# The turned rest's last 64 features on TensorE's two row halves, and a block's five down sums in an order set per block

## The chip, the cores and the metric

The kernel runs on one core of one Trainium2 chip. The metric is device time in microseconds (us) of one execution. The text uses the profiler's names for the engines: PE is TensorE's matmul path, PEld its weight loads, DVE is VectorE, ACT is ScalarE, POOL is GpSimd and SP is SyncE, which here only issues DMAs.

## What is computed

Two branches read the same input `x` of 2048 tokens by 640 features and are mixed by a gate of one number per token:

```python
x = A_x
g = _sigmoid((x * gate_w).sum(-1, keepdims=True))
a = _A_ref(x, A_wqkv, A_w_phi, A_wo)      # linear attention, 32 heads of 20
b = _B_ref(x, B_w_gate, B_w_up, B_w_down) # (silu(x @ w_gate) * (x @ w_up)) @ w_down
return g * a + (1 - g) * b
```

In `_A_ref`, q and k go through a small matrix per head and then through softmax(p) and softmax(-p), side by side. `kv` and `z` are sums over all tokens of phi_k times v and of phi_k; the output is phi_q times `kv`, divided by phi_q times `z`, and projected by `wo`. All inputs are bfloat16. The middle width of `_B_ref` is 1728 = 13 x 128 + 64, so its last slice of features has 64 rows instead of 128.

## The kernel before

**Tiles.** Tokens are handled in 16 tiles of 128 (attention) and in 4 blocks of 512 (`bt`, the feed-forward branch). The feed-forward's middle features are 14 slices (`k`): 13 of 128 and slice 13 of 64. A *pair* is the gate and the up matmuls of one slice of one block, five of 512 columns each (`ffn`). ACT then takes a tanh and a scaled copy out of PSUM, DVE multiplies into `hT` (line 690), and POOL multiplies by the copy (line 699, `hmul`). Slice 13 is stored folded: rows 0 to 63 of `hT[:, hb, 13, 0:256]` hold its 64 features for the block's tokens 0 to 255, rows 64 to 127 hold the same features for tokens 256 to 511.

**Down.** Each block has five sums over the 14 slices. Four (`down`, u = 0 to 3) give the first 512 output features of 128 tokens each. The fifth (`rest`) gives the last 128 output features of all 512 tokens, *turned*: features on partitions, tokens on columns; ACT copies it out and a DMA turns it back. Slices 0 to 12 are thirteen full-height matmuls per sum. Slice 13 is done for the four `down` sums by `edge`: four matmuls of 512 columns that use 64 rows each, in the order 0, 2, 1, 3, so that the upper and the lower row half of the PE array work side by side. The turned rest instead ends with two full-height matmuls of 256 columns whose weights are half zeros: `wd[:, 13, 512:640]` (zeros below) for tokens 0 to 255 and `wr` (zeros above) for tokens 256 to 511. A sum that stands ahead of `edge` is *early*: it starts the PSUM bank and `edge` closes it. The others are started by `edge`.

**Attention.** A *k tile* is fifteen matmuls of 460, 481 and 500 columns into a pair of PSUM banks and one bank more. DVE follows with a maximum (line 1057), a minimum (1061) and two subtractions (1065, 1069); the second subtraction gives the pair of banks back. ACT takes the exponential, DVE a sum (1080) and a reciprocal (1084), POOL normalises (1090). A *q tile* does the same with 480 columns, then a DMA turns it, `num` multiplies by the kv matrix, DVE divides (1192), another DMA turns, and `wo` projects.

**Order.** A planner in the kernel (`_Plan`) fixes the order of all engines while the program is built. It walks through planned time with a list per engine, sorted by priority, and starts the first task whose inputs, buffers and PSUM banks are ready by its own costs. Tasks can be held to a planned time: k tile `t` at `K_AT + K_EACH*t`, q tile `t` at `Q_AT + Q_EACH*t`. The DMAs that turn tiles are given an allowance on top of their planned landing (`E_SLACK`, `O_SLACK`). `downs_of` lists a block's sums and `D_AFTER` says behind which slice of a later block they stand. On the chip each engine works its list in order and waits on semaphores. `_Order` leaves out waits of PE on its own semaphore.

Line 466 is the helper through which nearly all matmuls go, line 476 the same for most of ACT's work.

Of the kernel before, what the change touches and what calls it, by code (L numbers as in the profile page):

```python
# [6 lines left out]
P = 128  # L7
S_TOK = 2048
D = 640
H = 32  # L10
DH = 20
F_FFN = 1728
NT = S_TOK // P
NBT = S_TOK // 512
NK = 14
# [31 lines left out]
BF16 = DT.bfloat16  # L47
# [204 lines left out]
class _Plan:  # L252
# [100 lines left out]
def _mm(*cols):  # L353
    return sum(c / 2400.0 + 0.003 for c in cols)


def _build(
# [34 lines left out]
    wkv = sb("wkv", [P, 5, KVW], BF16)  # L392
    wo = sb("wo", [P, 5, D], BF16)
    wd = sb("wd", [P, NK, D], BF16)
    wr = sb("wr", [P, P], BF16)
# [50 lines left out]
    def one(b, c0, c1, r0=0, r1=P):  # L446
        return ps[r0:r1, b * 512 + c0:b * 512 + c1]
# [4 lines left out]
    def mms(groups):  # L452

        reads = [g[1] for g in groups] + [g[2] for g in groups]
        writes = []
        seen = set()
        for g in groups:
            k = (g[0].offset, str(g[0].ap))
            if k not in seen:
                seen.add(k)  # L460
                writes.append(g[0])

        def fn():
            last = None
            for o, l, r, st, sp_ in groups:
                last = pe.matmul(o, lhsT=l, rhs=r, start=st, stop=sp_, skip_group_check=True)  # L466
            return last
        run("pe", fn, reads=reads, writes=writes)

    def acc(o, pairs):  # L470
        n = len(pairs)
# [33 lines left out]
    v1pad = v1all.rearrange("p (g x) -> p g x", x=WIN)[:, :, WIN - 1]  # L505

    DM = 512
    L_SLACK, E_SLACK, O_SLACK = 1.0, 1.8, 1.6
    chain = {}

    def load(eng, dst, src, land, prio, transpose=False, name="load", cost=0.06):

        t = add(eng, cost, lambda: dma(eng, dst, src, transpose=transpose), prio=prio, lat=2.0, name=name)
        t.land = land
        t.slack = L_SLACK if land > 13 else 0.0
        t.after = chain.get(eng)
        chain[eng] = t
        return t
# [75 lines left out]
    wqT_l = load_wT(0, 51.0, -26, range(4))  # L594
    wd_l = [load("sp", wd[:, 0:13, :], rows(B_w_down[0:13 * P, :]), 58.5, -25),
            load("sp", wd[0:64, 13, :], B_w_down[13 * P:F_FFN, :], 59.0, -24),
            load("sp", wd[64:P, 13, 0:DM], B_w_down[13 * P:F_FFN, 0:DM], 59.3, -23.9),
            load("sp", wr[64:P, :], B_w_down[13 * P:F_FFN, DM:D], 59.5, -23.8)]
    wo_l = load("sp", wo[:, :, :], rows(A_wo), 61.0, -23)
    xl = [x_[4] for x_ in xs]  # L600

# [3 lines left out]
    table = add("act", 1.3, lambda: actop(us[:, 1, 0:1], us[:, 0, 0:1], ACTF.Tanh), deps=[zero], prio=-20, name="table")  # L605
    ones_t = add("dve", 0.4, lambda: memset(v1ones, 1.0, "dve"), prio=-19)
    pads_t = add("dve", 0.2, lambda: memset(v1pad, 0.0, "dve"), prio=-18.5)
    for z_ in (wd[64:P, 13, DM:D], wr[0:64, :]):
        wd_l[3].deps.append(add("dve", 0.2, lambda z_=z_: memset(z_, 0.0, "dve"), prio=-18))

    def build_wbd(c):
        nh = PHI_NH[c]
# [155 lines left out]
    store_t = {}  # L768
    gs_t = {}
# [64 lines left out]

    rest_c = {}

    def edge(bt, rank):
        hb = bt % 2
        c_ = down_c[bt] = [{} for _ in range(4)]
        acq = [("bank", c_[u], "ps") for u in range(4) if u not in EARLY[bt]] + ([("bank", c_[3], "p2")] if bt == NBT - 1 else [])  # L840

        def tile(u, key="ps", c0=0, c1=DM):
            r0 = 64 * (u // 2)
            return (one(c_[u][key], 0, c1 - c0), hT[r0:r0 + 64, hb, 13, P * (u % 2):P * (u % 2) + P], wd[r0:r0 + 64, 13, c0:c1], u)

        def fn():
            last = [tile(3)] if bt < NBT - 1 else [tile(3, "ps", 0, 384), tile(3, "p2", 384, DM)]
            mms([(o, l, r, u not in EARLY[bt], u in EARLY[bt]) for o, l, r, u in [tile(0), tile(2), tile(1)] + last])
        edge_t[bt] = add("pe", 0.63, fn, deps=[mult_t[bt, 13]] + wd_l, prio=rank, acq=acq, name="edge")

    def rest(bt, rank):
        ctx = {}
        rest_c[bt] = ctx
        hb = bt % 2
        first = 4 * bt < B_FIRST

        def fn():
            o = one(ctx["ps"], 0, 512)
            mms([(o, wd[:, k, DM:D], hT[:, hb, k, :], k == 0, False) for k in range(13)] +
                [(o[:, 256 * i:256 * i + 256], l, hT[:, hb, 13, 0:256], False, True) for i, l in enumerate((wd[:, 13, DM:D], wr[:, :]))])  # L860
        rest_t[bt] = r_ = add("pe", _mm(*([512] * 13 + [256] * 2)), fn, deps=[mult_t[bt, k] for k in range(NK)] + wd_l, prio=rank,
                              acq=[("bank", ctx, "ps")], name="rest")

        def rcp():
            actop(xb[:, ctx["xb"], 0:512], one(ctx["ps"], 0, 512), ACTF.Copy)
        e = add("act", 0.49, rcp, deps=[r_], prio=1, acq=[("xb", ctx, "xb")], rel=[("bank", ctx, "ps")], name="rcp")
        xs_ = xsb[:, 4 * bt:4 * bt + 4, DM:D]

        def turn():
            dma("sp", xs_ if first else rX[:, ctx["rX"], :, :], xb[:, ctx["xb"], 0:512], transpose=True)  # L870
        x_ = add("sp", 1.3, turn, deps=[e, wq_done[0]], prio=0.5, lat=2.1, acq=() if first else [("rX", ctx, "rX")], rel=[("xb", ctx, "xb")], name="rX")
        x_.slack = E_SLACK
        if first:
            def scaled():
                g_ = gs[:, 1, 4 * bt:4 * bt + 4]
                poolop(lambda: pool.tensor_tensor(xs_, xs_, g_.unsqueeze(2).to_broadcast([P, 4, P]), ALU.mult), [xs_, g_], [xs_])
            x_ = add("pool", 1.1, scaled, deps=[x_, gs_t[bt]], prio=0.6, name="rsc")
        rest_x[bt] = x_

    def down(bt, u, rank):  # L880
        t = 4 * bt + u
        ctx = down_c[bt][u]
        hb = bt % 2
        early = u in EARLY[bt]
        tk = slice(P * u, P * u + P)

        def part(key, c0, c1):
            return lambda: mms([(one(ctx[key], 0, c1 - c0), hT[:, hb, k, tk], wd[:, k, c0:c1], early and k == 0, not early and k == 12) for k in range(13)])
        n = DM if t < NT - 1 else 384
        d_ = add("pe", _mm(*[n] * 13), part("ps", 0, n), deps=[mult_t[bt, k] for k in range(13)] + wd_l, prio=rank,  # L890
                 acq=[("bank", ctx, "ps")] if early else (), name="down")
        down_t[bt, u] = d_
        if early:
            edge_t[bt].deps.append(d_)
            return t, ctx, [(edge_t[bt], "ps", 0, n)]
        d_.deps.append(edge_t[bt])
        if n == DM:
            return t, ctx, [(d_, "ps", 0, n)]
        second = add("pe", _mm(*[DM - n] * 13), part("p2", n, DM), prio=0.0, name="down")
# [342 lines left out]
        for half in range(2):  # L1242
            kvpart(bt, half, 1.0)
    def downs_of(bt):
        e = [("d", u, bt) for u in range(4)]
        return [("r", 0, bt)] + e[0:2] + [("x", 0, bt)] + e[2:]
    seq = [("f", k, bt) for k in range(K_PAIRS) for bt in range(2) if bt or k >= HD]
    seq += [("f", k, 0) for k in range(K_PAIRS, NK)]
    for bt in range(1, NBT):
        for k in range(K_PAIRS if bt == 1 else 0, NK):  # L1250
            seq.append(("f", k, bt))
            if k == K_PAIRS * (bt == 1) + D_AFTER:
                seq += downs_of(bt - 1)[:1]
            if k == K_PAIRS * (bt == 1) + D_AFTER + 1:
                seq += downs_of(bt - 1)[1:]
    seq += downs_of(NBT - 1)
    downs = []
    for i, (kind, j, bt) in enumerate(seq):
        if kind == "f":
            ffn(bt, j, 10.0 + 0.01 * i)  # L1260
        elif kind == "r":
            rest(bt, 10.0 + 0.01 * i)
        elif kind == "d":
            if bt not in edge_t:
                edge(bt, 10.0 + 0.01 * seq.index(("x", 0, bt)))
            downs.append(down(bt, j, 10.0 + 0.01 * i))
    for t in range(NT):
        qtile(t, 5.0 + 0.01 * t)
# [56 lines left out]
```

## Time and profile before

| | |
|---|---|
| median of 3 runs | 286.21 us (286.15 to 286.26) |
| the profiled execution | 285.67 us, of which the span of the trace is 284.0 us |
| PE busy | 279.0 us (98% of the span) |
| DVE, POOL, ACT busy | 226.5, 166.8, 153.3 us |
| granted TensorE clock | 1.000 |

In the timeline a row merges like instructions that follow each other: start, length, engine, line, operation, output<-inputs, rows*columns of the array, shape, count. The end of a matmul is modelled and includes its way through the array, so that a row's length is longer than its share of PE: the distance between the starts of two rows is what PE spends on the first. Some matmul records are missing from the trace, and a row may then count one too few.

### The profile page before, as it was taken

What the parts mean: (1) busy time and instruction counts of PE and PEld (TensorE: products, weight loads), DVE (VectorE), ACT (ScalarE), POOL (GpSimd) and SP (SyncE); (2) the same over time, 40 slices, a digit from 0 to 9 for tenths busy, and PEclk for the clock granted to TensorE, in tenths of its full rate; (3) what the DMA queues carried; (4) which work ended last, traced back from release to release, by engine and by line L of the source; (5) the groups of instructions that cost most, each with busy time, mean ns of one, the idle gap of its engine ahead of it and who ended that gap; (6) DMA issues with size and microseconds to landing.
All of it is one profiled execution on the core that took longest, in us unless ns stands there. A gap on an engine that the chain in (4) does not pass through costs nothing.

```text
span 284.0 us, 4497 instructions
## 1 busy us (share of the span) xinstructions
PE 279.0 (98%) x1671; PEld 137.1 (48%) x1700; DVE 226.5 (80%) x334; ACT 153.3 (54%) x272; POOL 166.8 (59%) x140
## 2 busy tenths in 40 slices
PE   8999999999999999999999999999999999999996
PEld 3444544544544454455444455454554544454443
DVE  0324469999999999799989989999998999756114
ACT  2555746887765446676545554575435556635410
POOL 4198614677656744448765495687495686954200
PEclk9999999999999999999999999999999999999999
DMA  7988997957000100000011023332855553455012
GB/s 172 259 131 156 271 212 148 228 154 158 14 16 14 32 16 14 14 16 14 20 21 23 1 53 60 62 63 57 118 107 149 117 144 70 85 106 150 4 37 92
DMA packets 74591, 25.41 MB, mean 89 GB/s; under 512 B 62665, under 2 KB 74569, under 8 KB 74569
## 3 DMA queue, kind: packets, MB, share of 16 engines
q1 hardware_dynamic: 73257, 25.10, 40.8%
q8 instruction: 13, 0.21, 0.3%
q10 hardware_dynamic: 1312, 0.03, 0.3%
q14 instruction: 9, 0.07, 0.1%
HBM read 8.46 MB, written 2.62 MB: 39 GB/s over the span
## 4 chain that ended last, share of the span: by engine, by line
PE 89%; DVE 8%; issue 1%; ACT 1%; POOL 0%; POOLq 0%
PE ps L466 87%; PE ps L649 2%; DVE sm L1080 1%; DVE mx L1057 1%; DVE hT L690 1%; DVE phi L1065 1%; DVE phi L1069 1%; DVE ob L1192 1%; DVE mn L1061 1%; DVE rc L1084 1%; ACT us L694 0%; POOL hT L699 0%; ACT hT L476 0%; DVE rd L1184 0%; DVE dn L1182 0%
## 5 line engine op out<-in xcount | busy, mean ns | idle before, releaser
L699 POOL TENSOR_TENSOR hT<-hT,us 128x512 bf16<-128x512 bf16 (+1 forms) x56 | 62.4, 1121 | 61.9 <-DVE hT L690 35.4
L1090 POOL TENSOR_TENSOR phi<-phi,rc 128x1680 bf16<-128x1680 bf16 (+1 forms) x32 | 77.5, 2423 | 31.5 <-DVE rc L1084 31.4
L466 PE MATMUL ps<-xT,wg 128*128 128x512 bf16 (+1 forms) x285 | 65.9, 364 | 1.0 <-issue 0.2
L466 PE MATMUL ps<-xT,wu 128*128 128x512 bf16 x257 | 63.6, 379 | 0.2
L690 DVE SCALAR_TENSOR_TENSOR hT<-hT,ps 128x512 bf16<-128x512 bf16 (+1 forms) x60 | 38.4, 645 | 27.9 <-ACT hT L476 24.1
L476 ACT ACTIVATE hT<-ps 128x512 bf16<-128x512 f32 (+1 forms) x60 | 33.8, 567 | 36.4 <-PE ps L466 36.2
L466 PE MATMUL ps<-wkv,xT 128*128 128x460 bf16 (+2 forms) x240 | 51.1, 366 | 0.2 <-DVE phi L1069 0.2
L1080 DVE TENSOR_REDUCE sm<-phi 128x84 f32<-128x1680 bf16 (+1 forms) x32 | 48.3, 1513 | 2.0 <-ACT phi L476 2.0
L466 PE MATMUL ps<-wd,hT 128*128 128x512 bf16 (+3 forms) x231 | 48.3, 366 | 0.3
L476 ACT ACTIVATE phi<-phi 128x1680 bf16<-128x1680 bf16 (+1 forms) x32 | 41.7, 1302 | 7.2 <-DVE phi L1069 7.0
L466 PEld LDWEIGHTS ps<-xT,wg 128*128 128x128 bf16 x300 | 28.1, 98 | 29.2 <-issue 1.4
L694 ACT ACTIVATE us<-ps 128x512 bf16<-128x512 f32 (+1 forms) x60 | 33.9, 568 | 13.9 <-PE ps L466 12.8
L466 PEld LDWEIGHTS ps<-xT,wu 128*128 128x128 bf16 x260 | 25.3, 98 | 30.9 <-DMA wu<-in_B_w_up_dram 0.5
L466 PEld LDWEIGHTS ps<-wkv,xT 128*128 128x128 bf16 x240 | 23.2, 98 | 24.9 <-DVE phi L1069 0.7
L466 PEld LDWEIGHTS ps<-wd,hT 128*128 128x128 bf16 (+1 forms) x238 | 21.3, 98 | 25.1 <-issue 1.0
L1057 DVE TENSOR_REDUCE mx<-ps 128x42 f32<-128x840 f32 (+1 forms) x32 | 26.7, 833 | 7.6 <-PE ps L466 7.4
L1069 DVE TENSOR_TENSOR phi<-mn,ps 128x840 bf16<-128x840 f32 (+1 forms) x32 | 26.3, 821 | 0.3
L1061 DVE TENSOR_REDUCE mn<-ps 128x42 f32<-128x840 f32 (+1 forms) x32 | 26.5, 828 | 0.0
L1065 DVE TENSOR_TENSOR phi<-ps,mx 128x840 bf16<-128x840 f32 (+1 forms) x32 | 26.3, 822 | 0.0
L476 ACT ACTIVATE xb<-ps 128x512 bf16<-128x512 f32 x16 | 9.5, 595 | 19.7 <-PE ps L466 19.7
L466 PE MATMUL ps<-wo,oT 128*128 128x512 bf16 x77 | 19.2, 379 | 0.1
L466 PE MATMUL ps<-wq,xT 128*128 128x480 bf16 x80 | 18.7, 366 | 0.1
(64 smaller groups left out, 209.3 us busy)
## 6 DMA issues: line engine op xcount, KB each, us to landing
out_dram<-xsb SPq DMA_DIRECT2D x15, 160.0 KB, 1.9
wd<-in_B_w_down_dram SPq DMA_DIRECT2D x1, 2080.0 KB, 9.5
wg<-in_B_w_gate_dram SPq DMA_DIRECT2D x2, 400.0 KB, 6.3
wu<-in_B_w_up_dram SPq DMA_DIRECT2D x2, 400.0 KB, 7.3
wo<-in_A_wo_dram SPq DMA_DIRECT2D x1, 800.0 KB, 5.3
wg<-in_B_w_gate_dram SPq DMA_DIRECT2D x2, 320.0 KB, 4.3
wu<-in_B_w_up_dram SPq DMA_DIRECT2D x2, 320.0 KB, 4.9
wkv<-in_A_wqkv_dram SPq DMA_DIRECT2D x1, 600.0 KB, 8.0
```

The costliest lines, as they stand in the source:

```text
L466: last = pe.matmul(o, lhsT=l, rhs=r, start=st, stop=sp_, skip_group_check=True)
L476: run("act", lambda: act.activation(o, i, func, scale=scale), reads=reads, writes=[o])
L649: last = pe.matmul(one(b, 0, 512), lhsT=ones_row[:, 0:P], rhs=ones_row[:, 0:512], start=True, stop=True, skip_group_check=True)
L690: dveop(lambda: dve.scalar_tensor_tensor(out=h, in0=h, scalar=1.0, in1=g_, op0=ALU.add, op1=ALU.mult), [h, g_], [h])
L694: run("act", lambda: act.activation(o_, u_, ACTF.Copy, scale=0.5), reads=[u_], writes=[o_] if k < 13 else [o_, u_])
L699: poolop(lambda: pool.tensor_tensor(h, h, u_, ALU.mult), [h, u_], [h])
L1057: dveop(lambda: dve.tensor_reduce(a, b, AX.X, ALU.max), [b], [a])
L1061: dveop(lambda: dve.tensor_reduce(a, b, AX.X, ALU.min), [b], [a])
L1065: dveop(lambda: dve.tensor_tensor(o_, a, b, ALU.subtract), [a, mx[:, ctx["st"], 0:nh]], [o_])
L1069: dveop(lambda: dve.tensor_tensor(o_, a, b, ALU.subtract), [b, mn[:, ctx["st"], 0:nh]], [o_])
L1080: dveop(lambda: dve.tensor_reduce(a, b, AX.X, ALU.add), [b], [a])
L1090: poolop(lambda: pool.tensor_tensor(a, a, b, ALU.mult), [a, r], [a])
```

## The change

- `wr`, its load and the two DVE memsets of zeros are gone. `wd[64:128, 13, :]` now holds the last 64 rows of `w_down` in all 640 columns, by one load where there were two.
- The rest's two full-height matmuls of 256 columns are replaced by two of 256 columns on 64 rows, `turned(0)` and `turned(64)`, which join `edge`. Its order is now: turned(0) on the upper half; 2 (lower), 0 (upper), 3 (lower), 1 (upper); turned(64) on the lower half. In the last block tile 3 is split into 384 and 128 columns, as before.
- PE waits on its own semaphore for the end of `turned(0)` ahead of `turned(64)`, which writes the other half of the same PSUM bank.
- `rest` and `down` share a helper, `sums`. `SUMS` sets the order of the five sums (-1 is the rest) and of `edge` ("x") for each block. Before, the rest, 0 and 1 stood ahead of `edge`, and 2 and 3 behind; now 0 and the rest stand ahead.
- Constants of the planner move: `E_SLACK` 1.8 to 2.2, `O_SLACK` 1.6 to 1.9, the holds of k and q tiles, the times of the weight products (`PRE_...`), `D_AFTER` 1 to 3 with the whole of `downs_of` in one place. The order on every engine changes with them.

```diff
-    L_SLACK, E_SLACK, O_SLACK = 1.0, 1.8, 1.6
+    L_SLACK, E_SLACK, O_SLACK = 1.0, 2.2, 1.9
...
-            load("sp", wd[64:P, 13, 0:DM], B_w_down[13 * P:F_FFN, 0:DM], 59.3, -23.9),
-            load("sp", wr[64:P, :], B_w_down[13 * P:F_FFN, DM:D], 59.5, -23.8)]
+            load("sp", wd[64:P, 13, :], B_w_down[13 * P:F_FFN, :], 59.3, -23.9)]
...
-    for z_ in (wd[64:P, 13, DM:D], wr[0:64, :]):
-        wd_l[3].deps.append(add("dve", 0.2, lambda z_=z_: memset(z_, 0.0, "dve"), prio=-18))
...
-    K_AT, K_EACH, Q_AT, Q_EACH = 29.00, 6.821, 136.36, 6.844
-    PRE_Q = 10.07
-    PRE_EACH = 2.0
+    K_AT, K_EACH, Q_AT, Q_EACH = 30.00, 6.722, 137.19, 6.955
+    PRE_Q = 10.14
+    PRE_EACH = 2.3
     PRE_AT = 23.6
-    PRE_X = 27.5
-    D_AFTER = 1
+    PRE_X = 27.0
+    D_AFTER = 3
     FIN_DVE = 12
-    EARLY = ((0, 1),) * NBT
+    SUMS = ((0, -1, "x", 1, 2, 3), (0, -1, "x", 1, 2, 3), (-1, 0, "x", 1, 2, 3), (0, -1, "x", 2, 1, 3))
...
+        def turned(r0):
+            return (one(c_[-1]["ps"], 4 * r0, 4 * r0 + 256), wd[r0:r0 + 64, 13, DM:D], hT[r0:r0 + 64, hb, 13, 0:256], -1)
...
         def fn():
             last = [tile(3)] if bt < NBT - 1 else [tile(3, "ps", 0, 384), tile(3, "p2", 384, DM)]
-            mms([(o, l, r, u not in EARLY[bt], u in EARLY[bt]) for o, l, r, u in [tile(0), tile(2), tile(1)] + last])
-        edge_t[bt] = add("pe", 0.63, fn, deps=[mult_t[bt, 13]] + wd_l, prio=rank, acq=acq, name="edge")
+            done = halves([turned(0)])
+            halves([tile(2), tile(0), last[0], tile(1)] + last[1:])
+            pe.wait_ge(tr.sem["pe"], done[1])
+            halves([turned(64)])
+        edge_t[bt] = add("pe", 0.74, fn, deps=[mult_t[bt, 13]] + wd_l, prio=rank, acq=acq, name="edge")
...
-            mms([(o, wd[:, k, DM:D], hT[:, hb, k, :], k == 0, False) for k in range(13)] +
-                [(o[:, 256 * i:256 * i + 256], l, hT[:, hb, 13, 0:256], False, True) for i, l in enumerate((wd[:, 13, DM:D], wr[:, :]))])
+        rest_t[bt], r_ = sums(bt, -1, 512, lambda: [(one(ctx["ps"], 0, 512), wd[:, k, DM:D], hT[:, hb, k, :]) for k in range(13)], rank)
...
     def downs_of(bt):
-        e = [("d", u, bt) for u in range(4)]
-        return [("r", 0, bt)] + e[0:2] + [("x", 0, bt)] + e[2:]
+        return [("d", j, bt) for j in SUMS[bt]]
```

More of the change, by code (lines that the diff above doesn't have):

```diff
@@ L394, in _build @@
     wd = sb("wd", [P, NK, D], BF16)
-    wr = sb("wr", [P, P], BF16)
     wg = sb("wg", [P, 5, F_FFN + 128], BF16)
@@ L467, in fn @@
             return last
-        run("pe", fn, reads=reads, writes=writes)
+        return run("pe", fn, reads=reads, writes=writes)
     def acc(o, pairs):
@@ L835, in _build, with early @@
     rest_c = {}
+    def early(bt, j):
+        return SUMS[bt].index(j) < SUMS[bt].index("x")
     def edge(bt, rank):
         hb = bt % 2
-        c_ = down_c[bt] = [{} for _ in range(4)]
-        acq = [("bank", c_[u], "ps") for u in range(4) if u not in EARLY[bt]] + ([("bank", c_[3], "p2")] if bt == NBT - 1 else [])
+        c_ = down_c[bt] = {j: {} for j in range(-1, 4)}
+        acq = [("bank", c_[j], "ps") for j in range(-1, 4) if not early(bt, j)] + ([("bank", c_[3], "p2")] if bt == NBT - 1 else [])
+        def turned(r0):
+            return (one(c_[-1]["ps"], 4 * r0, 4 * r0 + 256), wd[r0:r0 + 64, 13, DM:D], hT[r0:r0 + 64, hb, 13, 0:256], -1)
         def tile(u, key="ps", c0=0, c1=DM):
@@ L844, in tile, with halves, sums, fn @@
             return (one(c_[u][key], 0, c1 - c0), hT[r0:r0 + 64, hb, 13, P * (u % 2):P * (u % 2) + P], wd[r0:r0 + 64, 13, c0:c1], u)
+        def halves(l):
+            return mms([(o, l_, r, not early(bt, j), early(bt, j)) for o, l_, r, j in l])
         def fn():
             last = [tile(3)] if bt < NBT - 1 else [tile(3, "ps", 0, 384), tile(3, "p2", 384, DM)]
-            mms([(o, l, r, u not in EARLY[bt], u in EARLY[bt]) for o, l, r, u in [tile(0), tile(2), tile(1)] + last])
-        edge_t[bt] = add("pe", 0.63, fn, deps=[mult_t[bt, 13]] + wd_l, prio=rank, acq=acq, name="edge")
+            done = halves([turned(0)])
[3 more added lines that the diff above has]
+        edge_t[bt] = add("pe", 0.74, fn, deps=[mult_t[bt, 13]] + wd_l, prio=rank, acq=acq, name="edge")
+    def sums(bt, j, n, groups, rank):
+        ctx = down_c[bt][j]
+        def fn():
+            mms([(o, l, r, early(bt, j) and k == 0, not early(bt, j) and k == 12) for k, (o, l, r) in enumerate(groups())])
+        t_ = add("pe", _mm(*[n] * 13), fn, deps=[mult_t[bt, k] for k in range(13)] + wd_l, prio=rank,
+                 acq=[("bank", ctx, "ps")] if early(bt, j) else (), name="down" if j >= 0 else "rest")
+        if early(bt, j):
+            edge_t[bt].deps.append(t_)
+            return t_, edge_t[bt]
+        t_.deps.append(edge_t[bt])
+        return t_, t_
     def rest(bt, rank):
-        ctx = {}
+        ctx = down_c[bt][-1]
         rest_c[bt] = ctx
@@ L855, in rest @@
         first = 4 * bt < B_FIRST
-        def fn():
-            o = one(ctx["ps"], 0, 512)
-            mms([(o, wd[:, k, DM:D], hT[:, hb, k, :], k == 0, False) for k in range(13)] +
-                [(o[:, 256 * i:256 * i + 256], l, hT[:, hb, 13, 0:256], False, True) for i, l in enumerate((wd[:, 13, DM:D], wr[:, :]))])
-        rest_t[bt] = r_ = add("pe", _mm(*([512] * 13 + [256] * 2)), fn, deps=[mult_t[bt, k] for k in range(NK)] + wd_l, prio=rank,
-                              acq=[("bank", ctx, "ps")], name="rest")
+        rest_t[bt], r_ = sums(bt, -1, 512, lambda: [(one(ctx["ps"], 0, 512), wd[:, k, DM:D], hT[:, hb, k, :]) for k in range(13)], rank)
         def rcp():
@@ L883, in down @@
         hb = bt % 2
-        early = u in EARLY[bt]
         tk = slice(P * u, P * u + P)
         def part(key, c0, c1):
-            return lambda: mms([(one(ctx[key], 0, c1 - c0), hT[:, hb, k, tk], wd[:, k, c0:c1], early and k == 0, not early and k == 12) for k in range(13)])
+            return [(one(ctx[key], 0, c1 - c0), hT[:, hb, k, tk], wd[:, k, c0:c1]) for k in range(13)]
         n = DM if t < NT - 1 else 384
[L890 to L896, printed above, removed]
+        down_t[bt, u], d_ = sums(bt, u, n, lambda: part("ps", 0, n), rank)
         if n == DM:
             return t, ctx, [(d_, "ps", 0, n)]
-        second = add("pe", _mm(*[DM - n] * 13), part("p2", n, DM), prio=0.0, name="down")
+        second = add("pe", _mm(*[DM - n] * 13), lambda: mms([(o, l, r, False, k == 12) for k, (o, l, r) in enumerate(part("p2", n, DM))]),
+                     prio=0.0, name="down")
         second.after = d_
@@ L1252, in _build @@
             if k == K_PAIRS * (bt == 1) + D_AFTER:
-                seq += downs_of(bt - 1)[:1]
-            if k == K_PAIRS * (bt == 1) + D_AFTER + 1:
-                seq += downs_of(bt - 1)[1:]
+                seq += downs_of(bt - 1)
     seq += downs_of(NBT - 1)
@@ L1260, in _build @@
             ffn(bt, j, 10.0 + 0.01 * i)
-        elif kind == "r":
-            rest(bt, 10.0 + 0.01 * i)
-        elif kind == "d":
+        else:
             if bt not in edge_t:
-                edge(bt, 10.0 + 0.01 * seq.index(("x", 0, bt)))
+                edge(bt, 10.0 + 0.01 * seq.index(("d", "x", bt)))
+            if j == "x":
+                continue
+            if j < 0:
+                rest(bt, 10.0 + 0.01 * i)
+                continue
             downs.append(down(bt, j, 10.0 + 0.01 * i))
```

## The prediction

> **What bounds the kernel now.** I read the page first, for the share of each engine:
>
> ```profile
> span 284.0 us, 4497 instructions
> PE 279.0 (98%) x1671; PEld 137.1 (48%) x1700; DVE 226.5 (80%) x334; ACT 153.3 (54%) x272; POOL 166.8 (59%) x140
> PEclk9999999999999999999999999999999999999999
> PE 89%; DVE 8%; issue 1%; ACT 1%; POOL 0%; POOLq 0%
> ```
>
> PE is busy for 279.0 of 284.0 us at full clock and has 89% of the chain that ended last. A saving must therefore be PE work removed or a PE stall removed; any other engine counts only where it makes PE wait. Next, the view of waits, for the stalls that are left:
>
> ```profile
> PE ps L466 <- DVE phi L1069: 0.2, 1, 0.2
> PEld ps L466 <- DMA wu<-in_B_w_up_dram: 0.5, 1, 0.5
> PEld ps L466 <- POOL hT L699: 0.4, 1, 0.4
> ```
>
> Three waits, and no more. A row's modelled end hides a part of a stall, so I take their size from the starts in the timeline. The first two rows below are the place of the DVE wait, the other four the place of the POOL wait at the end of the last block:
>
> ```profile
> 80.28 1.24 PE L466 MATMUL ps<-xT,wu 128*128 128x512 bf16 x5
> 81.69 3.22 PE L466 MATMUL ps<-wkv,xT 128*128 128x460 bf16 x15 [0.16 <-DVE phi L1069]
> ...
> 260.97 1.24 PE L466 MATMUL ps<-xT,wu 128*128 128x512 bf16 x5
> 262.05 1.24 PE L466 MATMUL ps<-wo,oT 128*128 128x512 bf16 x5
> 263.13 1.25 PE L466 MATMUL ps<-xT,wg 128*128 128x256 bf16 x10
> 264.50 2.98 PE L466 MATMUL ps<-wd,hT 128*128 128x512 bf16 x13
> ```
>
> Five matmuls of 512 columns take 1.08 us (262.05 - 260.97), 0.216 each. At 80.28 they take 1.41, so the eighth k tile waits 0.33 us for DVE's second subtraction of the sixth. The ten matmuls of 256 columns of slice 13 begin at 263.13; at 0.109 each (next part) the first down sum could start at 264.22 and starts at 264.50, a wait of 0.28 us for POOL's product of slice 12. Everywhere else the pitches hold, so PE's list is nearly a fixed sum of matmuls.
>
> **The two half-empty matmuls.** What goes, four times, is a pair of 256 columns:
>
> ```profile
> L466 PE MATMUL ps<-hT,wr 128*128 128x256 bf16 x4 | 1.1, 273 | 0.0
> L466 PE MATMUL ps<-hT,wd 128*128 128x256 bf16 x4 | 1.1, 272 | 0.0
> ...
> 133.96 0.27 PE L466 MATMUL ps<-hT,wr 128*128 128x256 bf16 x1
> 134.07 0.86 PE L466 MATMUL ps<-v,phi 128*128 128x64 bf16 x24
> ```
>
> One lasts 273 ns but holds PE for 0.11 (134.07 - 133.96), so two are worth 0.22 us a block. What comes instead is seen from the edge of block 1, which stands between a q tile and a gate; the two rows ahead of it give a q tile's pitch:
>
> ```profile
> 155.83 1.18 PE L466 MATMUL ps<-wq,xT 128*128 128x480 bf16 x5
> 156.84 0.38 PE L466 MATMUL ps<-wd,hT 128*128 128x512 bf16 x1
> ...
> 149.21 1.18 PE L466 MATMUL ps<-wq,xT 128*128 128x480 bf16 x5
> 150.32 0.61 PE L466 MATMUL ps<-wd,hT 64*128 64x512 bf16 x4
> 150.85 1.25 PE L466 MATMUL ps<-xT,wg 128*128 128x512 bf16 x5
> ...
> L466 PE MATMUL ps<-wd,hT 64*128 64x512 bf16 x15 | 2.4, 382 | 0.0
> ```
>
> A q tile takes 1.01 us, so edge could start at 150.22 and starts at 150.32: 0.10 to enter the halves. The row of four lasts 0.61 and one alone 0.38, so the second pair starts 0.23 after the first: two pairs stream for about 0.45. The next full matmul starts at 150.85, 0.08 after that. Edge costs 0.63 in all. With the change each half streams 1280 columns (256 + 512 + 512 above, 512 + 512 + 256 below) instead of 1024: 0.11 more, one entry and one exit as before, 0.74. Per block -0.22 + 0.11 = -0.11 us, over four blocks **-0.44 us**. More than that isn't there, since both halves are full from end to end.
>
> Less is possible in two ways. First, the pieces no longer start in equal pairs. That halves needn't be in step shows in the last block, where 384 and 128 columns below lie beside 512 above:
>
> ```profile
> 275.40 0.33 PEld L466 LDWEIGHTS ps<-wd,hT 64*128 64x128 bf16 x5 [0.42 <-issue]
> 275.94 0.55 PEld L466 LDWEIGHTS ps<-wd,hT 128*128 128x128 bf16 x4 [0.21 <-issue]
> ...
> 108.19 0.12 PEld L466 LDWEIGHTS ps<-wd,hT 64*128 64x128 bf16 x4
> ```
>
> From the first row-half load to the next full load it takes 0.54 us, as against 0.53 (150.32 to 150.85) for four equal pieces: the split cost nothing. The last row shows that all four weights of an edge are loaded within 0.12 us, while the first pair, 0.22 long, still streams. The Trainium skill says otherwise (TensorE: Matmul & The Clock Gate, The mechanism): a weight load overlaps with matmuls in flight only where its row group differs from theirs, by which each further piece on a half would show its load. The trace disagrees, since the second pair starts 0.23 and not 0.33 us after the first.
>
> Second, the new wait. PE waits on `turned(0)`, and behind it stand `turned(64)` and everything else of PE's list. How soon the end of a matmul of 256 columns is seen:
>
> ```profile
> 271.31 0.27 PE L466 MATMUL ps<-hT,wr 128*128 128x256 bf16 x1
> 271.62 0.60 ACT L476 ACTIVATE xb<-ps 128x512 bf16<-128x512 f32 x1 [2.43 <-PE ps L466]
> ```
>
> ACT starts 0.31 us after that matmul's start. `turned(64)` comes up when `tile(1)` has begun, 0.11 + 0.22 = 0.33 after `turned(0)`, and the lower half is free for it at 0.44. So the wait should be over when PE reaches it, with 0.02 to 0.13 us to spare, and I take it at nothing. At worst it shows a bare weight load, the 0.10 of the entry, which would eat the whole 0.11 of its block.
>
> **The two waits that go.** They are not the change's subject, but it moves the order. The order as built puts, between the last up group of block 3 and its first down sum, a `num` (eleven short matmuls), two `wo` groups and slice 13: more than 2 x 1.08 + 1.09 = 3.25 us of PE, where there was one `wo` group and slice 13, 2.17. What POOL's product needs:
>
> ```profile
> 262.25 0.60 ACT L694 ACTIVATE us<-ps 128x512 bf16<-128x512 f32 x1 [0.48 <-PE ps L466]
> 263.30 1.15 POOL L699 TENSOR_TENSOR hT<-hT,us 128x512 bf16<-128x512 bf16 x1 [2.71 <-ACT us L694]
> ```
>
> From the end of the up group (262.05) over ACT's copy and POOL's product (to 264.45) to PE's start at 264.50 it takes 2.45 us. With 0.8 us to spare the wait is gone: **-0.28 us**. Were ACT or POOL later by more than that, the old price would be back; behind it the next late thing is the edge's need of slice 13, which has the sum of 0, that of the rest and a `wo` group ahead of it.
>
> The DVE wait, on the k tiles numbered from 0:
>
> ```profile
> 68.58 3.21 PE L466 MATMUL ps<-wkv,xT 128*128 128x460 bf16 x15
> 119.56 3.21 PE L466 MATMUL ps<-wkv,xT 128*128 128x460 bf16 x15
> 122.60 2.33 PE L466 MATMUL ps<-xT,wg 128*128 128x256 bf16 x15
> 71.83 1.03 DVE L1057 TENSOR_REDUCE mx<-ps 128x42 f32<-128x840 f32 x1
> 72.78 1.02 DVE L1061 TENSOR_REDUCE mn<-ps 128x42 f32<-128x840 f32 x1
> 80.61 1.02 DVE L1069 TENSOR_TENSOR phi<-mn,ps 128x840 bf16<-128x840 f32 x1
> 81.55 0.68 DVE L690 SCALAR_TENSOR_TENSOR hT<-hT,ps 128x512 bf16<-128x512 bf16 x1
> 82.15 1.02 DVE L1061 TENSOR_REDUCE mn<-ps 128x42 f32<-128x840 f32 x1
> 86.55 0.97 DVE L1069 TENSOR_TENSOR phi<-mn,ps 128x840 bf16<-128x840 f32 x1
> ```
>
> A k tile holds PE for 3.04 us (122.60 - 119.56). Before, k tile 5 starts at 68.58, its maximum at 71.83, and its second subtraction ends at 81.63: 9.8 us of DVE work, with the maximum of k tile 6 (0.95, from 71.83 to 72.78) within. In the new order that maximum stands behind, which leaves 8.85. Adding the pitches of the new PE order, with the DMA wait at the head kept, k tile 5 starts near 70.1; its maximum can start 3.25 us later as before, at 73.4, so the subtraction ends at 82.2. Between the two k tiles the order has one more k tile, two pairs, slice 13, both kv halves and a weight product, 13.0 us, so PE comes to k tile 7 at 83.1. It is 0.9 us early where it was 0.33 late: **-0.33 us**.
>
> What is late next is k tile 8, which waits for k tile 6's second subtraction. Before, 5.9 us lie between the ends of these two subtractions (81.63 to 87.52). The new order has two maxima and two products of line 690 more between them (0.95 and 0.60 each, the latter from 81.55 to 82.15): 9.0 us, which ends at 91.2, or up to 0.7 earlier as far as the gaps between rows in the older stretch close. PE gets there after another k tile, two pairs and two weight products, 7.8 us behind k tile 7: 90.9. That is 0.4 early to 0.3 late. So a new wait of 0 to 0.3 us is likely here, and I take **+0.15 us**, the middle, as nothing speaks for one end. Elsewhere on this path the new order leaves more: k tiles 9 to 11 and 13 to 15 stand 13 us and more behind the k tile whose banks they need, and k tile 12, at 8.9 us, comes when DVE has worked off its backlog, as 12 us without a new k tile lie ahead of k tile 10.
>
> **What costs nothing.** One load and two memsets go; the loads of `w_down` still stand ahead of the same work, first used 7 us later in the new order, and DVE's memsets stand at the very head, before its first product. The weight products for q move behind later pairs but number the same. The rest is now closed by edge, so its copy and its turn on SP's queue start later; in the last block a `wo` group and 52 matmuls of three sums still follow it on PE. q tiles start 2 to 3 us later (the first at 152.0 for 149.2), and so do `num` groups, but by the pitches the last q tile keeps its distance to its `num`, and the last `num` gets 0.7 us more to its `wo`. The end behind PE's last matmul (one DVE product, one store) is untouched.
>
> **Sum.** -0.44 - 0.28 - 0.33 + 0.15 = -0.90 us. The profiled execution of 285.67 us would become 284.77; it lies 0.54 below the median of 286.21, which I carry over: **285.3 us**. About 0.2%, 0.57 us, is what a measurement of this kernel can tell from no change, so 285.64 is the border to faster.
>
> **The rivals.** *The forecast* holds where edge saves its 0.44 and new waits stay below 0.47: 285.1 (none) to 285.64. Chance 0.67.
>
> *The waits only move.* DVE is busy for 80% of the span and paces the k tiles, q tiles start later with the same work behind, and any stretch may hold a new wait like the two that go. For it: the margin at k tile 8 is about nil. Against: the list of waits shows only these in 284 us, and turned tiles have larger allowances. With 0.61 us of new waits it is 286.21 - 0.44 = 285.77, the same by measurement; 286.1 with half as much again. Chance 0.16.
>
> *Weights of a half load in the open.* If the new order of unequal pieces loses the early loading, each half shows two loads of 0.10: edge is 0.94, the block loses 0.09, and with the waits as forecast it is 285.3 + 4 x 0.20 = 286.1. This is what the Trainium skill's rule above would do here. Against it stand the 0.12 us of the four loads and the unsplit cost of the last block. Chance 0.05.
>
> *The halves take turns.* If pieces overlap only where they start together, no two of the six do, since `turned(0)` shifts the upper half by 0.11. Then edge is 2560 columns in a row, 5 x 0.216 + 0.18 = 1.26, and a block loses 0.63 + 0.63 - 0.85 = 0.41 in place of gaining 0.11. Four times 0.52 on the forecast: 287.4, slower. It decides from 0.37 us per edge on. Against it: the last block's unequal edge of 0.54. Chance 0.07; another 0.05 for slower by several small things.
>
> **How the numbers follow.** Faster 0.67, same 0.16 + 0.05 = 0.21, slower 0.12. The range: below, 285.16 with no new wait, less a little for the spread of runs, 285.0; above, it takes in the moved waits and the open loads, 286.2, which leaves out the slower cases and little else.
>
> **What would show it.** Right: edge rows of six with 0.73 to 0.75 us from the pitch end before them to the next full matmul, and `wr` gone; no POOL wait near 264; the k tile near 83 unstalled; PE's list of waits of 0.5 us or less beside the one for the first `wu`. Wrong: a next full matmul 0.8 us or more behind the edge's first; a wait on PE's own semaphore with idle weight loads ahead of the last piece; rows of k tiles, `num` or `wo` with DVE, POOL or DMA as their releaser, which would say that the waits moved.

## The result, and the profile after

| | before | changed |
|---|---|---|
| median | 286.18 us (285.77 to 286.78, 10 runs) | 285.46 us (285.03 to 285.64, 10 runs) |
| ratio, 95% interval | | 0.9973 [0.9963, 0.9983] |
| the profiled execution | 285.67 us, span 284.0 | 285.48 us, span 283.7 |

The changed kernel is faster by 0.72 us (0.49 to 1.06 by the interval). A second measurement of it, further down, gives 0.9978 [0.9969, 0.9988]. The profiled execution itself is shorter by only 0.2 us, and that has to be explained as well.

In the changed kernel the line numbers are a little different: the helper for matmuls is line 465 (466 before), ACT's is 475, `hmul` is 695, DVE's second subtraction is 1078, its last products are 795 and 814 (799 and 818 before). SPq is SP issuing DMAs. First lines of the page of the changed kernel, and of its lists of waits for PE and for the weight loads:

```profile
span 283.7 us, 4489 instructions
PE 278.8 (98%) x1671; PEld 137.2 (48%) x1700; DVE 225.9 (80%) x332; ACT 152.5 (54%) x272; POOL 166.4 (59%) x140
PEclk9999999999999999999999999999999999999999
PE 98%; issue 1%; DVE 0%
...
PE ps L645 <- PEq L1318: 0.8, 1, 0.8
...
PEld ps L465 <- ACT us L690: 0.7, 2, 0.4
```

The chain that ended last passes through DVE only with the last product (0%) and no longer through POOL. PE's own list has one entry left, ahead of the first real matmul; the kernel before has the same one. A weight load that waits need not hold PE, so the waits that remain are read from the starts. First the edge of block 1, which now follows k tile 15, with the weight load of its last piece:

```profile
145.25 3.20 PE L465 MATMUL ps<-wkv,xT 128*128 128x460 bf16 x15
148.39 0.28 PE L465 MATMUL ps<-hT,wd 64*128 64x256 bf16 x1
148.39 0.71 PE L465 MATMUL ps<-wd,hT 64*128 64x512 bf16 x4
148.84 0.27 PE L465 MATMUL ps<-hT,wd 64*128 64x256 bf16 x1
149.04 2.76 PE L465 MATMUL ps<-wd,hT 128*128 128x512 bf16 x11
...
148.73 0.09 PEld L465 LDWEIGHTS ps<-hT,wd 64*128 64x128 bf16 x1
```

The k tile holds PE for 3.04 us, to 148.29. `turned(0)` starts 0.10 later, and the next full matmul at 149.04: the edge costs 0.75 by these rows, 0.74 by the unrounded starts, and 0.74 to 0.75 in each of the four blocks. `turned(64)`, the second row of 256 columns, starts at 148.84, 0.45 after `turned(0)`, which is when its half comes free. Its weights were loaded at 148.73, while the piece ahead of it on the same half still streamed.

Then the two places where PE stalled before, k tile 7 (and k tile 8, where a new wait was feared), with the DVE subtractions that give their banks back (and the maximum of k tile 5 ahead of them), and the end of block 3:

```profile
82.38 1.24 PE L465 MATMUL ps<-xT,wu 128*128 128x512 bf16 x5
83.46 3.20 PE L465 MATMUL ps<-wkv,xT 128*128 128x460 bf16 x15
...
90.19 1.24 PE L465 MATMUL ps<-xT,wu 128*128 128x512 bf16 x5
91.27 3.21 PE L465 MATMUL ps<-wkv,xT 128*128 128x460 bf16 x15
...
73.72 1.03 DVE L1066 TENSOR_REDUCE mx<-ps 128x42 f32<-128x840 f32 x1 [1.19 <-PE ps L465]
80.77 1.02 DVE L1078 TENSOR_TENSOR phi<-mn,ps 128x840 bf16<-128x840 f32 x1
89.67 1.02 DVE L1078 TENSOR_TENSOR phi<-mn,ps 128x840 bf16<-128x840 f32 x1
...
262.99 1.26 PE L465 MATMUL ps<-xT,wg 128*128 128x256 bf16 x10
264.09 2.75 PE L465 MATMUL ps<-wd,hT 128*128 128x512 bf16 x12
```

Both up groups ahead of the k tiles take their plain 1.08 us: no wait. The subtractions end at 81.79 and 90.69, 1.7 and 0.6 us before PE needs the banks. The ten matmuls of 256 columns at 262.99 take 1.10, so the first down sum follows without a wait. What is left in the middle is small:

```profile
170.42 1.18 PE L465 MATMUL ps<-wq,xT 128*128 128x480 bf16 x5
171.53 0.56 PEld L465 LDWEIGHTS ps<-xT,wg 128*128 128x128 bf16 x4 [0.40 <-ACT us L690]
171.56 1.24 PE L465 MATMUL ps<-xT,wg 128*128 128x512 bf16 x5
```

A q tile holds PE for 1.01 us; this one 1.14, so the gate behind it waits 0.13 for ACT's copy to give its bank back. With 0.06 near 63.9 and 0.05 near 266.9, found in the same way, that makes 0.24 us, where there was 0.33 + 0.28 = 0.61.

The end is where something was lost. DVE's last products and SP's last stores, of the changed kernel:

```profile
278.48 0.75 DVE L795 SCALAR_TENSOR_TENSOR xsb<-ps,gs,xsb 128x512 bf16<-128x512 f32 x1 [2.05 <-PE ps L465]
279.14 1.13 DVE L814 SCALAR_TENSOR_TENSOR xsb<-rX,gs,xsb 128x128 bf16<-128x128 bf16 x4
280.59 1.08 DVE L795 SCALAR_TENSOR_TENSOR xsb<-ps,gs,xsb 128x384 bf16<-128x384 f32 x2 [0.32 <-PE ps L465]
279.51 2.77 SPq L493 DMA_DIRECT2D out_dram<-xsb  x6
281.36 0.92 SPq L493 DMA_DIRECT2D out_dram<-xsb  x2
```

and of the kernel before:

```profile
277.38 0.60 DVE L818 SCALAR_TENSOR_TENSOR xsb<-rX,gs,xsb 128x128 bf16<-128x128 bf16 x2
281.07 1.08 DVE L799 SCALAR_TENSOR_TENSOR xsb<-ps,gs,xsb 128x384 bf16<-128x384 f32 x2 [0.84 <-PE ps L466]
277.75 4.77 SPq L494 DMA_DIRECT2D out_dram<-xsb  x6
281.71 0.81 SPq L494 DMA_DIRECT2D out_dram<-xsb  x2
```

In each of the two, the second SPq row is the last two of the six stores in the first. Before, the six were spread over 4.77 us, and the last was issued 0.37 us after DVE's last product (282.52 against 282.15). In the changed kernel the four products with `rX` stand behind the final product of tile 13 in DVE's list, and the first of the six stores leaves only at 279.51. From there SP issues them back to back, 0.46 us each, and the last is out 0.61 us after DVE's last product (282.28 against 281.67). So the end became 0.24 us longer; counted from PE's last matmul to the end of the span it is 0.25.

Lastly the head. The gate of the third pair of slices has the same matmuls ahead of it in both kernels; the row of before comes first, that of the changed kernel second:

```profile
13.76 1.24 PE L466 MATMUL ps<-xT,wg 128*128 128x512 bf16 x5
```

```profile
14.07 1.24 PE L465 MATMUL ps<-xT,wg 128*128 128x512 bf16 x5
```

In this execution of the changed kernel that gate starts 0.31 us later. The page rounds the spans to a tenth; to two digits they end at 283.95 and 283.72 us. So from that row to the end of the span it is 270.19 us before and 269.65 after, 0.54 less. With the 0.31 of the head this leaves 0.23, which is the 0.2 by which the profiled execution is shorter. The second measurement's profile has that row at 13.87 and ends at 283.52, which is 269.65 again. The head varies from execution to execution; the rest was the same in these two, so I compare experiments from that row on ("behind the head"), with each span's end to two digits.

### The profile page after: what moved, and what is told of

It is laid out like the page before. It is cut to its first block, busy times and chain, and to the rows that moved or that the text cites. A ratio compares the mean times of both kernels' runs of the same rounds, so it can differ in the third digit from the quotient of the medians.

```text
span 283.7 us, 4489 instructions
## 1 busy us (share of the span) xinstructions
PE 278.8 (98%) x1671; PEld 137.2 (48%) x1700; DVE 225.9 (80%) x332; ACT 152.5 (54%) x272; POOL 166.4 (59%) x140
## 4 chain that ended last, share of the span: by engine, by line
PE 98%; issue 1%; DVE 0%
PE ps L465 97%; PE ps L645 2%; DVE xsb L795 0%
## 5 line engine op out<-in xcount | busy, mean ns | idle before, releaser
L465 PE MATMUL ps<-xT,wg 128*128 128x512 bf16 (+1 forms) x287 | 67.2, 366 | 0.8
L465 PE MATMUL ps<-wd,hT 128*128 128x512 bf16 (+4 forms) x230 | 48.6, 366 | 0.4
L690 ACT ACTIVATE us<-ps 128x512 bf16<-128x512 f32 (+1 forms) x60 | 33.7, 567 | 13.6 <-PE ps L465 12.3
L807 POOL TENSOR_TENSOR xsb<-xsb,xb 128x512 bf16<-128x512 bf16 x12 | 13.8, 1151 | 13.4 <-ACT xb L475 13.4
```

Source lines behind the costliest of these rows:

```text
L690: run("act", lambda: act.activation(o_, u_, ACTF.Copy, scale=0.5), reads=[u_], writes=[o_] if k < 13 else [o_, u_])
L807: poolop(lambda: pool.tensor_tensor(x_, x_, b_, ALU.add), [x_, b_], [x_])
```

## The experiments

The theory: the gain is the four shorter edges (0.44) and the waits that the new order removes (0.61 less 0.24), less 0.25 at the end behind PE's last matmul; the wait on PE's own semaphore is free only because it stands ahead of the last piece. Against it: the gain is all order and the edge does nothing, or the other way about; and the wait costs something already. The next four kernels ran on one chip, on which the kernel before has a median of 285.91 us (24 runs); each ratio is to it.

**The pair back, the order kept.** Slice 13 of the turned rest is again two full-height matmuls with `wr`, directly ahead of an edge of four pieces. The load and the memsets come back with it. The planner still counts 0.74 for both, so that everything else keeps its place.

```diff
...
-            done = halves([turned(0)])
-            halves([tile(2), tile(0), last[0], tile(1)] + last[1:])
-            pe.wait_ge(tr.sem["pe"], done[1])
-            halves([turned(64)])
+            o = one(c_[-1]["ps"], 0, 512)
+            mms([(o[:, 256 * i:256 * i + 256], l, hT[:, hb, 13, 0:256], not early(bt, -1), early(bt, -1)) for i, l in enumerate((wd[:, 13, DM:D], wr[:, :]))])
+            halves([tile(0), tile(2), tile(1)] + last)
```

> The changed kernel with one part undone: the turned rest's slice 13 is again two full-height matmuls of 256 columns with half-zero weights, now directly ahead of an edge of four row-half matmuls. The planner's cost of edge is left, so that PE's list outside edge is the changed kernel's. Theory (the row halves save 0.11 us a block, the new order removes two waits): edge and pair take 0.85 us a block instead of 0.74, so the kernel is 0.4 us slower than the changed one (about 285.9) and still about 0.3 us faster than the one before. Rival A (the order does it all, the halves give nothing): equal to the changed kernel, 285.5. Rival B (the halves do it all): equal to the one before, 286.2.

Measured: 286.08 us (285.67 to 286.36, 11 runs), ratio 1.0000 [0.9992, 1.0009]: the time of the kernel before. The edge of block 1 in its timeline, weight loads last:

```profile
148.20 0.27 PE L466 MATMUL ps<-hT,wd 128*128 128x256 bf16 x1
148.31 0.27 PE L466 MATMUL ps<-hT,wr 128*128 128x256 bf16 x1
...
148.51 0.11 PEld L466 LDWEIGHTS ps<-wd,hT 64*128 64x128 bf16 x4 [0.21 <-issue]
149.04 1.41 PEld L466 LDWEIGHTS ps<-wd,hT 128*128 128x128 bf16 x8 [0.42 <-issue]
```

From the pair's start to the next full weights it is 0.84, and the pair itself starts without an entry: 0.85 per block against 0.74. The small waits of 0.24 and the longer end are those of the changed kernel. Its terms add up to -0.61 + 0.24 + 0.25 = -0.12 against the kernel before. The trace has just that: behind the head it takes 270.07 us (span to 283.94, the third pair's gate at 13.86), 0.12 less than the kernel before. The interval (-0.23 to +0.26 us) can't tell it from nothing, so the 0.3 that was expected over the kernel before isn't there, and by the times alone rival B would fit. The trace rules it out: the two waits are gone here too, and the end and the small waits take back most of what that gives. The merged edge turns it into a gain: behind the head this kernel takes 0.42 us more than the changed one, close to 4 x 0.11. The times put the two further apart, by 0.6 to 0.8 us, but with 0.4 either way, and they were not measured side by side; the 0.42 stands by the traces.

**The planner's constants of before.** Edge, `SUMS` and `D_AFTER` as changed; the allowances, the holds and the times of the weight products as before.

```diff
-    L_SLACK, E_SLACK, O_SLACK = 1.0, 2.2, 1.9
+    L_SLACK, E_SLACK, O_SLACK = 1.0, 1.8, 1.6
...
-    K_AT, K_EACH, Q_AT, Q_EACH = 30.00, 6.722, 137.19, 6.955
-    PRE_Q = 10.14
-    PRE_EACH = 2.3
+    K_AT, K_EACH, Q_AT, Q_EACH = 29.00, 6.821, 136.36, 6.844
+    PRE_Q = 10.07
+    PRE_EACH = 2.0
...
-    PRE_X = 27.0
+    PRE_X = 27.5
```

> The changed kernel with only the planner's constants put back to the values of before (holds of k and q tiles, times of the weight products, the two allowances); edge, SUMS and the place of the sums stay as changed. The planner makes another order of it. Theory: each edge still takes 0.74 us, and the total depends on new waits of PE alone: 285.2 without any, 285.8 with as many as before, more if the last block is hit. Rival (the gain of 0.4 us comes with the halves whatever the order): 285.5 to 285.8. If it is over 286.2, a good order is worth more than the halves.

Measured: 288.90 us (288.61 to 289.17, 4 runs), ratio 1.0105 [1.0090, 1.0120], slower by 3.0 us. Two places of its timeline carry that:

```profile
254.19 1.25 PE L465 MATMUL ps<-xT,wg 128*128 128x256 bf16 x10
256.36 2.98 PE L465 MATMUL ps<-wd,hT 128*128 128x512 bf16 x13 [0.91 <-POOL hT L695]
...
280.49 1.19 SPq L493 DMA_TRANSPOSE xsb<-xb  x1
281.98 1.08 DVE L795 SCALAR_TENSOR_TENSOR xsb<-ps,gs,xsb 128x384 bf16<-128x384 f32 x2 [2.44 <-PE ps L465]
282.98 1.13 DVE L814 SCALAR_TENSOR_TENSOR xsb<-rX,gs,xsb 128x128 bf16<-128x128 bf16 x4
282.63 2.78 SPq L493 DMA_DIRECT2D out_dram<-xsb  x6
```

Ten matmuls of 256 columns take 1.10, so the first down sum of the last block waits 1.07 us for POOL (256.36 less 255.29). With 0.46 and 0.33 elsewhere and a few small ones, PE stalls for 2.0 us in place of 0.24. And the turn of a last rest is issued only at 280.49, so that four products and the stores stand behind PE's last matmul: SP ends 2.35 us after DVE's product of the last tile, where it was 0.61. The two make 1.8 + 1.7 = 3.5 us over the changed kernel, and behind the head it is 3.6 (286.89 less 13.66, against 269.65). The theory counted on waits of PE alone and had no price for the end, which is half of the loss. So the edge still costs 0.74 here, but the order around it loses several times what it saves. This is not the order of the kernel before, since `SUMS` and `D_AFTER` are the changed kernel's; the merged edge in the whole order of before was not run. Which of the constants matters most was not separated.

**The place of the wait.** Two kernels with less work between `turned(0)` and `turned(64)`: in the first `turned(64)` moves to the middle (turned(0), 2, 0, wait, turned(64), 1, 3), in the second `turned(0)` moves to the end, directly ahead of it (0, 2, 1, 3, turned(0), wait, turned(64)).

```diff
             done = halves([turned(0)])
-            halves([tile(2), tile(0), last[0], tile(1)] + last[1:])
+            halves([tile(2), tile(0)])
             pe.wait_ge(tr.sem["pe"], done[1])
             halves([turned(64)])
+            halves([tile(1)] + last)
```

> The changed kernel with turned(64) moved up within edge: turned(0), 2, 0, the wait, turned(64), then 1 and 3. Nothing else moves. It shows whether the wait is free only because of its place. Each half still streams 1280 columns. Theory: turned(64) could start when tile 2 leaves the lower half, 0.22 us after turned(0), but the end of turned(0) is seen at 0.29 to 0.31 and the weights come after that, so the lower half stands for 0.1 to 0.2 us: edge 0.85 to 0.95, the kernel 0.4 to 0.8 us slower than the changed one. Rival (the wait costs nothing, wherever it stands, or weights load ahead of it): 0.74 an edge, the same time.

```diff
+            halves([tile(0), tile(2), tile(1)] + last)
             done = halves([turned(0)])
-            halves([tile(2), tile(0), last[0], tile(1)] + last[1:])
             pe.wait_ge(tr.sem["pe"], done[1])
             halves([turned(64)])
```

> The changed kernel with turned(0) moved behind the four tiles of edge, next to turned(64), so that the wait is fully exposed: 0, 2, 1, 3, turned(0), the wait, turned(64). Theory: turned(0) starts 0.45 us into the stretch, its end is seen 0.29 to 0.31 later, then come a weight load of 0.1 and 0.11 of columns: 0.10 + 0.45 + 0.30 + 0.10 + 0.11 + 0.08 = 1.14 us an edge, 0.4 more than now, 1.6 us in all: 287.0, slower than before the change. Rival (the wait is free): 0.74 to 0.85 an edge, within 0.4 us of the changed kernel.

Measured: 285.79 us (285.56 to 286.41, 12 runs), ratio 0.9999 [0.9991, 1.0007], in the middle; 286.73 us (286.39 to 287.24, 7 runs), ratio 1.0028 [1.0016, 1.0039], at the end. The weight loads of the edge of block 1, first of the kernel with the middle place, then with the last:

```profile
148.14 0.09 PEld L465 LDWEIGHTS ps<-hT,wd 64*128 64x128 bf16 x1 [0.41 <-issue]
148.14 0.11 PEld L465 LDWEIGHTS ps<-wd,hT 64*128 64x128 bf16 x2
148.48 0.09 PEld L465 LDWEIGHTS ps<-hT,wd 64*128 64x128 bf16 x1 [0.23 <-PE ps L465]
148.91 1.63 PEld L465 LDWEIGHTS ps<-wd,hT 128*128 128x128 bf16 x9 [0.32 <-issue]
```

```profile
149.17 0.11 PEld L465 LDWEIGHTS ps<-wd,hT 64*128 64x128 bf16 x4 [0.41 <-issue]
149.40 0.09 PEld L465 LDWEIGHTS ps<-hT,wd 64*128 64x128 bf16 x1
149.94 0.09 PEld L465 LDWEIGHTS ps<-hT,wd 64*128 64x128 bf16 x1 [0.45 <-PE ps L465]
150.16 0.33 PEld L465 LDWEIGHTS ps<-wd,hT 128*128 128x128 bf16 x3
```

Now the wait shows, with PE's own matmul as its releaser. In the middle `turned(64)` gets its weights 0.34 us after `turned(0)` got its own, and everything behind it stands back; the edge grows from 0.74 to 0.86 (0.87 by these rows). At the end the wait stands bare: `turned(64)` starts 0.33 us after `turned(0)` started, and the edge is 1.08. So PE's wait on a matmul of 256 columns takes 0.33 us from that matmul's start to the start of the dependent one. Behind the head (the third pair's gate at 13.70 and 14.52, the spans' ends at 283.84 and 285.51) the two take 270.13 and 270.99 us, 0.48 and 1.34 over the changed kernel; four edges, each longer by 0.12 and 0.34, would be 0.48 and 1.36. Placed in the middle, the wait eats the whole gain of the merged edge; placed last, three times that.

**The changed kernel once more**, beside the next one, on another chip than the four above.

> The changed kernel once more, beside the next one on the same chip. In its profile the six last stores are issued by SP back to back from 279.5 us, 0.43 to 0.46 each, and the last one 0.5 us behind the DVE product that it waits for, and PE's last matmul lies 2.6 us before the end of the span. All that should be seen again. The start of the stretch behind the first loads may move by some tenths from one execution to the next.

Measured: 285.29 us (285.03 to 285.92, 11 runs) against 285.90 (285.48 to 286.61, 18 runs), ratio 0.9978 [0.9969, 0.9988]. In its profile SP's last six stores again follow each other, for 2.78 us from 279.31.

**The end mended.** The planner expects the turned rests later than they land by its allowance `E_SLACK`, and therefore places DVE's products with them late. Without the allowance for the last block's two turns (the same edit at both places that issue them) only the last entries of DVE's and SP's lists change places.

```diff
-        x_.slack = E_SLACK
+        x_.slack = E_SLACK if bt < NBT - 1 else 0.0
```

> The changed kernel with one thing more: the allowance on the two DMAs that turn the last block's rests is 0 in place of 2.2 in the plan. Only the last lists change: DVE does the four products of the last 128 features (xsb<-rX) ahead of the final product of tile 13 and not behind it, and SP gets the stores of tiles 12 and 14 and of the last 128 features earlier. Theory (the new order pays 0.25 us at the end, as six stores stand in SP's queue when the last one is wanted): PE's last matmul lies 2.36 us before the end of the span, as before the change, and the kernel is 0.2 to 0.25 us faster than the changed one. Rival (the end is longer for another reason, as the landing of the last store): 2.6 us as now, and the same time.

Measured: 285.01 us (284.74 to 285.50, 8 runs), ratio 0.9969 [0.9959, 0.9980]. Its end:

```profile
276.30 1.13 DVE L814 SCALAR_TENSOR_TENSOR xsb<-rX,gs,xsb 128x128 bf16<-128x128 bf16 x4
280.55 1.08 DVE L795 SCALAR_TENSOR_TENSOR xsb<-ps,gs,xsb 128x384 bf16<-128x384 f32 x2 [1.36 <-PE ps L465]
276.67 5.33 SPq L493 DMA_DIRECT2D out_dram<-xsb  x6
281.19 0.81 SPq L493 DMA_DIRECT2D out_dram<-xsb  x2
```

The four products start at 276.30 in place of 279.14, the stores are spread over 5.33 us, and the last issue ends 0.37 us after the last product (282.00 against 281.63), as in the kernel before. Behind the head (from 14.03 to 283.43) it takes 269.40, 0.25 less than the changed kernel, as expected. The medians differ by 0.28 us; their intervals against the kernel before overlap, so it is the trace that shows the size. By median and by trace this is the fastest of the versions that were run.

## Why the prediction was right, and where it was not

The total was near: 285.3 us forecast, 285.46 and 285.29 measured in two places, with the sign and the two main causes as forecast. In part that is luck. The medians moved by 0.72 and 0.61 us, but the work behind the head shrank by 0.54 and not by 0.90; with 0.54 the forecast would have been 285.67, just above its own border to faster. The terms, one by one:

- **The edge, -0.44: right.** 0.74 us by the trace for 0.74 forecast, and 0.85 for edge and pair with the pair put back. The row 148.39 with the next full matmul at 149.04 is what was named as the sign.
- **Weights of a half: right, and the halves don't take turns.** With loads in the open the edge would be 0.94, with halves in turn 1.26. The Trainium skill (TensorE: Matmul & The Clock Gate, The mechanism) lets a weight load overlap with a matmul in flight only where its row group differs. Taken alone, that rule is contradicted here once more, in unequal pieces: the load at 148.73 runs while its own half streams, and the six loads of one edge cost nothing beyond the entry. The same section of the Trainium skill also lets a load into the background weight buffer be pulled ahead, which the prediction left out. The trace agrees with that: 148.73 is 0.11 ahead of the piece it is for.
- **The wait on PE's own semaphore, 0: right,** and by the margin that was given: the path of 0.33 us from the start of `turned(0)` ends 0.11 to 0.12 before the half comes free at 0.45, where 0.02 to 0.13 was forecast. That it is free because of its place, and not because such waits are, the two moved kernels show.
- **The POOL wait, -0.28, and the DVE wait, -0.33: right.** Both are gone, with 1.7 us to spare at k tile 7 for the 0.9 forecast. The view of waits has more entries than the three of the prediction, such as `PEld ps L466 <- ACT gtan L989: 0.9, 3, 0.3`, but by the starts only these two hold PE behind the head. The new order alone keeps them away too, as the kernel with the pair shows; with the older constants, the wait for POOL is back at 1.07 us.
- **The wait at k tile 8, +0.15: not there.** The subtraction ended at 90.69, within what was given (91.2 or up to 0.7 earlier), but not for the reason given, that gaps close between the two subtractions: that stretch took 8.90 us for the 9.0 forecast. DVE was early ahead of it. From k tile 5's maximum (73.72) to its second subtraction's end (81.79) it took 8.07 us and not 8.85, for the most part because one product of 0.59 us that stands there in the kernel before (`75.53 0.68 DVE L690 SCALAR_TENSOR_TENSOR hT<-hT,ps 128x512 bf16<-128x512 bf16 x1`) does not in the new order, which the forecast did not take off. And PE came 0.37 later than forecast (91.27 for 90.9), about as much as the head. In place of this wait there are three small ones of 0.24 in places that were not named, so that the allowance for new waits was nearly the right size for the wrong reason.
- **The end behind PE's last matmul, 0: wrong.** The step said that it is "untouched", one product and one store. The product and the store are the same, but the store's place in SP's queue isn't: it now stands behind five others that leave back to back. The step looked at what the last store needs and not at what is queued ahead of it, though the text itself lists SP's queue and the later turn of the rest. Measured: +0.24 us, and the mended kernel, in which only the last products and stores change places, gets 0.25 back.

With these the sum is -0.44 - 0.61 + 0.24 + 0.25 = -0.56 us in place of -0.90; behind the head the traces show -0.54. The first interval, -0.49 to -1.06, holds both sums, the second, -0.34 to -0.89, the mended one and just not the other. So 0.34 us of the forecast's 0.90, over a third, did not come, which is near the limit of what the measurement can tell. That the profiled execution itself became 0.2 us shorter and not 0.5 is the 0.31 of its head; a forecast from one execution carries that much of the head's chance with it.

The rival by which *the waits only move* was right about the new order by itself, which without the merged edge brings nothing that can be measured, but wrong about how: half of what is given back, the 0.25 at the end, is not a wait of PE, and so it doesn't show in the lists of waits that were to give it away.

## What to carry to other kernels

After a change of order, price the end of the kernel as its own stage: list what each queue still has to issue after the last matmul, with what stands ahead of it in that queue, and not just what the last item depends on. PE's wait on its own semaphore took 0.33 us here where it stood bare and cost nothing behind 0.45 us of other pieces, so put independent work of that length between the two, and look at which place hides it. A saving of a tenth of a microsecond per block shows only in an order that doesn't stall elsewhere: here the same edge with the older constants of the planner was 3.0 us slower than the kernel before.

## What was not expected of the hardware

- The issue of a store holds SP for 0.33 us where SP was idle before it (the store at 279.99 in the kernel before), and six that follow each other take 0.46 each on average (279.51 to 282.28).
- The two row halves run independently in pieces of unequal length: 256, 512 and 512 columns beside 512, 512 and 256 leave no gap on either half. By their unrounded starts the pieces begin 0, 0.12 and 0.34 us into the edge of block 1 on the upper half, and 0, 0.23 and 0.45 on the lower. Of the 0.74 us in all, 1280 columns at 0.216 per 512 are 0.54, entering is 0.10 and leaving about 0.10.
- Executions of one kernel differ by 0.6 to 1.1 us (285.03 to 285.64 for the changed kernel in one set of runs, 285.48 to 286.61 for the kernel before in another). In the profiled ones the third pair's gate starts between 13.66 and 14.52, while the time behind it was the same in the two profiles of the changed kernel (269.65).
